# First mixture layer computed from packed rows times w_in, on one core of a Trainium2 chip

## The chip, the core and the metric

One Trainium2 chip, one of its cores. The metric is device time of one execution in microseconds (us); the time of a kernel is the median of its runs. Five engines work side by side, each through its own list in order: PE (TensorE, matmuls; its weight loads are shown as PEld), DVE (VectorE), ACT (ScalarE), POOL (GpSimd) and SP (SyncE, which here issues all transfers).

## What is computed

Attention goes through 32 packed rows per head, twice a softmax; then come two dense mixture layers over 2304 tokens. All is float32, but w_in and w_out arrive as float64.

```python
def sm_attn(qq, kk, vv):
    s = scale * np.matmul(qq, kk.transpose(0, 1, 3, 2))
    s = s - np.max(s, axis=-1, keepdims=True)
    a = np.exp(s)
    a = a / (np.sum(a, axis=-1, keepdims=True) + 1e-09)
    return np.matmul(a, vv)
p_packed = sm_attn(p, k, v)                # (4, 8, 32, 64)
out = sm_attn(q, p_packed, p_packed)       # (4, 8, 576, 64)
x = out.transpose(0, 2, 1, 3).reshape(2304, 512)
h = x @ w_in                               # (512, 2048)
g = h * (1.0 / (1.0 + np.exp(-1.702 * h)))
x = g @ w_out                              # (2048, 512)
p = domain_probs / (domain_probs.sum(-1, keepdims=True) + 1e-09)
for e in range(4):
    h = np.maximum(x @ w1[e], 0.0)         # (512, 1024)
    out2 += p[:, e:e + 1] * (h @ w2[e])    # (1024, 512)
```

## The kernel before

**Attention** is done in eight units, one per batch and group of four heads. `pack(u)` (L230) transposes k, takes scores of the packed rows (L253), the maximum and exponential (L260, L266), transposes the exponentials (L280), multiplies by v (L287) and leaves in `pp` the packed rows, once transposed (L308) and once block-diagonal over head pairs (L300). `unpack(u)` (L312) transposes q, takes scores (L324), the softmax over 32 packed rows (L335 to L343), and multiplies the softmax weights with the packed rows (L348, float32, 288 columns, two records each in the trace). The result is x, features on partitions.

**Precision.** Every large matrix is kept as two parts, high and low, whose sum is the float32 value. A product of the MoE layers is three products: high x high, low x high, high x low (`PARTS`, L17). The split is a rounding copy on ACT and a subtraction. A float64 weight is first turned into float32 by six DVE steps (L155, L156, L160, L166, L169, L172) and one POOL step (L163) for each piece of 128x512; 32 pieces in all. This is called a conversion below. The low part (L99) is made by POOL for the first pass and by DVE later.

**MoE layers.** Tokens are in five blocks (four of 512 columns, one of 256). A pass takes four chunks of 128 hidden columns through all blocks: 4 passes for the first layer, 8 for the second. `f1(i)` (L375) is the first product of a step: 12 matmuls (4 contraction tiles x 3 parts), then the activation on ACT (L397) and the high and low parts on DVE (L398, L399); `f2(i)` (L408) is the second: 12 matmuls into four accumulators (L420, in the second layer L428), added to the block's sum at the pass's end (L454, L465). They are issued as f1(i+1), f2(i), f1(i+2), f2(i+1), so each activation has a step of the other kind as cover.

**Order.** The word list `PROG` (L24) issues loads, stages of pack and unpack, weight fetches (F), conversions (C) and MoE halves (M), and a scheduler sets the order on each engine from it. After the head, `WHEN` (L537) says after which steps the next pass's weights are converted. All loads are on SP, in order; a weight load waits for one of two raw buffers. PSUM has 8 banks, taken in turn.

## Time and profile before

| | |
|---|---|
| runs | 1314.97, 1315.67, 1318.59 us; median 1315.67 |
| profiled execution, span | 1313.9 us from its first to its last instruction; the profile gives no other time of this execution |
| TensorE busy | 1282.4 us, 98% of the span |
| VectorE, ScalarE, GpSimd busy | 524.4, 291.0, 81.8 us |
| mean granted TensorE clock | 0.989 of full speed |
| moved by DMA | 53.71 MB |

The busy time of TensorE is the time with a matmul under way, and a matmul that waits for its predecessor in the array counts as busy. So how fast matmuls follow each other is read from the starts in the timeline, not from the length of one. Idle time of an engine matters only where another one waits for it.

### The profile page before, as it was taken

Reading aid. Unit: us, or ns where it says so; the run is one execution under the profiler, and the core shown is the slowest. Engines: PE = TensorE matmul, PEld = TensorE weight load, DVE = VectorE, ACT = ScalarE, POOL = GpSimd, SP = SyncE. Lnnn points to the kernel's source line nnn. Section 1 sums busy time; section 2 is a strip of 40 time slices with the busy share of each in tenths; the row PEclk is TensorE's granted clock in tenths of the full one; section 3 lists DMA queues with packets and bytes.
Section 4 is the critical chain, followed back from the end, with each engine's and each line's share of the span. In section 5 each row is a group of like instructions: output and inputs, shape, how many; then the busy total and the mean of one; then the engine's idle time right before and its main releaser. Section 6 shows DMA issues by size and latency. Waiting matters only on the chain.

```text
span 1313.9 us, 15157 instructions
## 1 busy us (share of the span) xinstructions
PE 1282.4 (98%) x6400; PEld 1051.0 (80%) x6400; DVE 524.4 (40%) x952; ACT 291.0 (22%) x552; POOL 81.8 (6%) x74
## 2 busy tenths in 40 slices
PE   5699999999999999999999999999999999999998
PEld 4477787888888888888888888888888888888887
DVE  5985559639534453112224223223224224123222
ACT  3555542112111221322112112012112112111110
POOL 2410002101000232000000000000000000000000
PEclk7899999999999999999999999999999999999999
DMA  9662013102101001012001002002002001000011
GB/s 237 164 160 56 19 33 112 49 1 96 32 1 33 0 33 32 0 33 65 0 0 65 0 1 65 0 0 65 0 1 64 0 0 54 11 1 0 33 64 48
DMA packets 79365, 53.71 MB, mean 41 GB/s; under 512 B 43201, under 2 KB 70849, under 8 KB 79297
## 3 DMA queue, kind: packets, MB, share of 16 engines
q1 hardware_dynamic: 79296, 52.74, 14.0%
q8 instruction: 50, 0.82, 0.3%
q14 instruction: 19, 0.15, 0.0%
HBM read 48.01 MB, written 4.72 MB: 40 GB/s over the span
## 4 chain that ended last, share of the span: by engine, by line
PE 92%; DVE 4%; DMA 1%; SPq 1%; POOL 1%; ACT 1%; issue 0%; ACTq 0%; POOLq 0%
PE ps_h L384 45%; PE ps_acc L428 30%; PE ps_acc L420 14%; PE ps_t L220 1%; PE ps_o L348 1%; PE ps_s L324 1%; SPq L212 1%; DVE man L172 1%; DVE ex L169 1%; DMA raw<-in_moe_w_out_dram 0%; POOL ex L163 0%; DVE ex L155 0%; DMA v<-in_v_dram 0%; DMA raw<-in_moe_w_in_dram 0%; DVE w L99 0%
## 5 line engine op out<-in xcount | busy, mean ns | idle before, releaser
L428 PE MATMUL ps_acc<-w,h 128*128 128x512 f32 x1728 | 428.1, 395 | 0.0
L428 PEld LDWEIGHTS ps_acc<-w,h 128*128 128x128 f32 x1728 | 323.6, 189 | 72.7
L402 DVE SCALAR_TENSOR_TENSOR h<-ps_h,h 128x512 fp32r<-128x512 f32 (+1 forms) x160 | 102.2, 639 | 528.9 <-ACT h L401 528.9
L384 PE MATMUL ps_h<-yh,w 128*128 128x512 f32 x1024 | 256.5, 392 | 0.0
L384 PEld LDWEIGHTS ps_h<-yh,w 128*128 128x128 f32 x1024 | 192.3, 188 | 44.4
L401 ACT ACTIVATE h<-ps_h 128x512 fp32r<-128x512 f32 (+1 forms) x160 | 88.8, 555 | 616.1 <-PE ps_h L384 616.1
L420 PE MATMUL ps_acc<-h,w 128*128 128x512 f32 (+1 forms) x960 | 219.8, 375 | 1.5 <-DVE h L398 0.8
L420 PEld LDWEIGHTS ps_acc<-h,w 128*128 128x128 f32 x960 | 167.2, 188 | 38.2 <-DVE h L399 1.7
L384 PE MATMUL ps_h<-yl,w 128*128 128x512 f32 x512 | 137.8, 391 | 0.0
L384 PE MATMUL ps_h<-xh,w 128*128 128x512 f32 x512 | 131.6, 397 | 0.4 <-DVE pp L300 0.4
L384 PEld LDWEIGHTS ps_h<-yl,w 128*128 128x128 f32 x512 | 96.1, 188 | 20.4
L384 PEld LDWEIGHTS ps_h<-xh,w 128*128 128x128 f32 x512 | 95.0, 189 | 21.1 <-PE ps_pt L307 0.7
L397 ACT ACTIVATE g<-ps_h 128x512 f32<-128x512 f32 (+1 forms) x80 | 44.4, 555 | 222.1 <-PE ps_h L384 212.1
L398 DVE CAST h<-g 128x512 fp32r<-128x512 f32 (+1 forms) x80 | 35.5, 444 | 136.7 <-ACT g L397 136.6
L465 DVE SCALAR_TENSOR_TENSOR acc<-ps_acc,pr,acc 128x512 f32<-128x512 f32 x126 | 86.4, 743 | 2.2 <-PE ps_acc L428 2.2
L384 PE MATMUL ps_h<-xl,w 128*128 128x512 f32 x256 | 69.8, 394 | 0.0
L99 DVE TENSOR_TENSOR w<-raw,w 128x1024 fp32r<-128x1024 f32 x32 | 41.7, 1308 | 52.0 <-ACT w L98 52.0
L384 PEld LDWEIGHTS ps_h<-xl,w 128*128 128x128 f32 x256 | 48.5, 190 | 10.3
L399 DVE TENSOR_TENSOR h<-g,h 128x512 fp32r<-128x512 f32 (+1 forms) x80 | 53.5, 669 | 1.6
L384 PEld LDWEIGHTS ps_h<-y,w 128*128 128x128 f32 x384 | 50.3, 191 | 2.8
L384 PE MATMUL ps_h<-y,w 128*128 128x256 f32 x384 | 51.0, 283 | 0.0
L163 POOL TENSOR_SCALAR ex<-ex 128x512 uint32<-128x512 uint32 x32 | 33.4, 1043 | 187.7 <-DVE ex L160 187.6
(82 smaller groups left out, 649.7 us busy)
## 6 DMA issues: line engine op xcount, KB each, us to landing
raw<-in_moe_w_dram SPq DMA_DIRECT2D x64, 256.0 KB, 3.0
raw<-in_moe_w_in_dram SPq DMA_DIRECT2D x16, 512.0 KB, 3.7
raw<-in_moe_w_out_dram SPq DMA_DIRECT2D x16, 512.0 KB, 3.7
k<-in_k_dram SPq DMA_DIRECT2D x32, 144.0 KB, 4.1
v<-in_v_dram SPq DMA_DIRECT2D x8, 576.0 KB, 6.5
q<-in_q_dram SPq DMA_DIRECT2D x32, 144.0 KB, 4.3
out_dram<-acc SPq DMA_DIRECT2D x18, 256.0 KB, 2.0
praw<-in_p_dram SPq DMA_DIRECT2D x1, 256.0 KB, 3.1
```

The lines of the kernel that those rows point to most:

```text
L99: eng.tensor_sub(out=dst[:, 1, :], in0=src, in1=dst[:, 0, :].bitcast(F32))
L163: nc.gpsimd.tensor_scalar(out=ex, in0=ex, scalar1=-float(896 << 20), scalar2=8.0, op0=ALU.add, op1=ALU.mult)
L169: nc.vector.scalar_tensor_tensor(out=ex, in0=hi, scalar=0x80000000, in1=ex, op0=ALU.bitwise_and, op1=ALU.bitwise_or)
L384: nc.tensor.matmul(out=ps[:, :n], lhsT=w[:, wp, kk * 128:(kk + 1) * 128], rhs=x[xp][:, kk, :], start=(m == 0), stop=(m == 3 * KD - 1),)
L397: nc.scalar.activation(out=g32[:, :n], in_=ps[:, :n], func=AF.Gelu_apprx_sigmoid)
L398: nc.vector.tensor_copy(out=h[:, 0, :n], in_=g32[:, :n])
L399: nc.vector.tensor_sub(out=h[:, 1, :n], in0=g32[:, :n], in1=h[:, 0, :n].bitcast(F32))
L401: nc.scalar.activation(out=h[:, 0, :n], in_=ps[:, :n], func=AF.Relu)
L402: nc.vector.scalar_tensor_tensor(out=h[:, 1, :n], in0=ps[:, :n], scalar=0.0, in1=h[:, 0, :n].bitcast(F32), op0=ALU.max, op1=ALU.subtract,)
L420: nc.tensor.matmul(out=accs[j][t][:, :n], lhsT=w[:, wp, 512 + t * 128:512 + (t + 1) * 128], rhs=h[:, hq, :n], start=(c == 0 and m == 0), s ...
L428: nc.tensor.matmul(out=accs[j][t], lhsT=h[:, hq, t * 128:(t + 1) * 128], rhs=w[:, wp, 512:1024], start=(c == 0 and m == 0), stop=(c == CPP ...
L465: nc.vector.scalar_tensor_tensor(out=acc[:, t, :], in0=ps[t], scalar=pr[:, tok, e:e + 1], in1=acc[:, t, :], op0=ALU.mult, op1=ALU.add,)
```

## The change

Since x = A P (A the softmax weights, P the packed rows, block-diagonal over the heads), x w_in = A (P w_in). For each pass and batch, `packed_w` multiplies the transposed block-diagonal packed rows of a unit with 512 columns of w_in; the result, split in two parts, is the stationary operand of `l1_first`, whose moving operand is A^T (four heads x 32 rows = 128 partitions per unit, two units). So a step's first product has 6 matmuls in place of 12, and L348 and its splits go; A is split instead (`split` in `unpack`). The first layer works in eight half-batches of 288 tokens in place of five blocks; the second layer keeps its blocks, and `put_y` writes the first layer's result into them. ACT makes the activation twice (into the rounded high part, and in float32) and DVE only the low part.

All eight packs are in the list ahead of the first MoE step; units 2 to 7 are unpacked beside the first layer's first pass. Slots are 36 small ones instead of 20 large ones, raw buffers three instead of two; w_in is fetched in rows of 512 columns. POOL takes over the low part of every converted piece, the mask product of p, the subtraction of the maximum in `unpack`, and the low parts of the packed rows. In the second layer the next pass's weights are converted after other steps (`WHEN`).

```diff
-    "k0 k1 F F v0 q0 v1 S P1 P0 P1 P1 q1 P0 C P0 P1 P0 P1 P0 P0 P1 P1 P0 k2 v2 C U1 k3 v3 q2 P2 P3 C U0 "
...
+    "k0 k1 S v0 v1 P0 P1 k2 k3 P0 P1 F P0 P1 F v2 v3 P0 P1 P0 P1 C P2 P3 k4 k5 P0 P1 P2 P3 C F v4 v5 P0 P1 P2 P3 C "
...
-    big = ctx.enter_context(tc.tile_pool(name="big", bufs=20))
+    big = ctx.enter_context(tc.tile_pool(name="big", bufs=36))
-    rawp = ctx.enter_context(tc.tile_pool(name="rawp", bufs=2))
+    rawp = ctx.enter_context(tc.tile_pool(name="rawp", bufs=3))
+    cv = ctx.enter_context(tc.tile_pool(name="cv", bufs=2))
...
-        split_w(w[:, :, s * 512:(s + 1) * 512], f32, aux)
+        split(w[:, 0, :], w[:, 1, :], f32, nc.gpsimd)
...
-        nc.vector.scalar_tensor_tensor(
-            out=pp[:, 2:4, :].rearrange("p j (a d) -> p (j a) d", a=2),
...
+        pw = ppws[b][:, g]
+        nc.gpsimd.memset(pw.bitcast(F32), 0.0)
+        for j in range(2):
+            cs = slice(64 * j, 64 * j + 64)
+            split(pw[:, j, 0, cs], pw[:, j, 1, cs], ppT[:, cs], nc.gpsimd)
...
-        nc.vector.tensor_sub(out=t, in0=t, in1=s2[:, 0, :].unsqueeze(2).to_broadcast([128, NB, NP]))
+        nc.gpsimd.tensor_sub(out=t, in0=t, in1=s2[:, 0, :].unsqueeze(2).to_broadcast([128, NB, NP]))
...
+        A[u] = slot([128, 2, S], F32R, f"a{u}")
+        split(A[u][:, 0, :], A[u][:, 1, :], aT, nc.vector)
...
-                nc.tensor.matmul(
-                    out=ps[:, :HS], lhsT=pp[:, 2 + j, :], rhs=aT[:, s * HS:(s + 1) * HS], start=True, stop=True
-                )
...
+    def packed_w(a, b):
+        for g in range(UG):
...
+            for j in range(2):
+                for wp, xp in PARTS:
+                    nc.tensor.matmul(
+                        out=ps, lhsT=pw[:, j, wp, :], rhs=W["in", a, 2 * g + j][:, xp, :],
...
+            split(PW[a, b, g][:, 0, :], PW[a, b, g][:, 1, :], ps, nc.vector)
...
+    def l1_first(a, j, c):
...
+        for wp, xp in PARTS:
+            for g in range(UG):
+                nc.tensor.matmul(
+                    out=ps[:, :HS],
+                    lhsT=PW[a, b, g][:, wp, c * 128:(c + 1) * 128],
+                    rhs=A[b * UG + g][:, xp, s * HS:(s + 1) * HS],
...
+        nc.scalar.activation(out=h[:, 0, :HS], in_=ps[:, :HS], func=AF.Gelu_apprx_sigmoid)
+        nc.scalar.activation(out=g32, in_=ps[:, :HS], func=AF.Gelu_apprx_sigmoid)
+        nc.vector.tensor_sub(out=h[:, 1, :HS], in0=g32, in1=h[:, 0, :HS].bitcast(F32))
...
-    WHEN = ((2, 0), (2, 3), (4, 1), (4, 2))
+    WHEN = ((2, 0), (4, 0), (4, 1), (4, 2))
```

The order on the engines, at three places (a name after the line number is what is written, those behind the arrow what is read).

PE around the first MoE product, before: v products of units 2 and 3 (L287), their last transposes (L307), then the first step of f1 (L384).

```order
L287 MATMUL ps_v<-v_304,k_299 32x64 x24
L287 MATMUL ps_v<-v_335,k_330 32x64 x24
L307 MATMUL ps_pt<-ident,pp_342 128x128
L384 MATMUL ps_h<-xh_548,w_169 128x512 x6
L307 MATMUL ps_pt<-ident,pp_348 128x128
```

The same place now: the last scores of units 6 and 7 (L235), the packed rows times w_in (L347), the exponentials of units 6 and 7 (L262), then their v products (L269); `l1_first` (L362) comes behind those.

```order
L347 MATMUL ps_w<-win,ppw_387 128x512
L235 MATMUL ps_s<-kT_899,pT_811 64x288
L347 MATMUL ps_w<-win,ppw_387 128x512 x5
L262 MATMUL ps_e<-ident,E_988 96x128 x6
L262 MATMUL ps_e<-ident,E_1002 96x128 x6
L347 MATMUL ps_w<-win,ppw_387 128x512 x6
L269 MATMUL ps_v<-v_639,k_539 32x64 x2
```

Four more packs stand ahead of the first product than before.

DVE in the first layer, before, in a stretch with conversions: each L398/L399 pair is an activation's two parts, L99 the low part of a piece of weights.

```order
L99 TENSOR_TENSOR w7_2102<-man_2103,w7_2102 128x512
L169 SCALAR_TENSOR_TENSOR ex_2117<-raw7_1_2070,ex_2117 128x512
L398 CAST h_2142<-g32_2143 128x512
L172 SCALAR_TENSOR_TENSOR man_2116<-man_2116,ex_2117 128x512
L399 TENSOR_TENSOR h_2142<-g32_2143,h_2142 128x512
L398 CAST h_2172<-g32_2173 128x512
```

The same engine now, in a middle pass, behind a packed product (pw0 and pw1 are its low parts, L374 the low part of an activation, L419 the sum of a half-batch, the rest conversion).

```order
L91 TENSOR_TENSOR pw0_2636<-ps_w_2629,pw0_2636 128x512
L91 TENSOR_TENSOR pw1_2646<-ps_w_2639,pw1_2646 128x512
L157 TENSOR_SCALAR man_3010<-raw_2627 128x512
L374 TENSOR_TENSOR h_2656<-g32_2657,h_2656 128x288
L166 SCALAR_TENSOR_TENSOR man_3010<-raw_2627,man_3010 128x512
L157 TENSOR_SCALAR man_3128<-raw_2765 128x512
L172 SCALAR_TENSOR_TENSOR man_3010<-man_3010,ex_3011 128x512
L419 TENSOR_TENSOR acc1_1582<-ps_acc_2575,acc1_1582 128x288
L374 TENSOR_TENSOR h_2680<-g32_2681,h_2680 128x288
```

Steps of two conversions stand between the activations' low parts; L157 writes a buffer that POOL's subtraction of an earlier piece has read.

ACT while queries are unpacked beside the first layer, now (L372 and L373 the two activations, L321 the exponential of a unit, L208 copies of transposed queries).

```order
L208 COPY qT_1159<-ps_t 128x288 x2
L208 COPY qT_1176<-ps_t 128x288 x2
L90 CAST win<-man 128x512
L372 ACTIVATE h<-ps_h 128x288
L373 ACTIVATE g_1262<-ps_h 128x288
L321 ACT_TABLE_LOAD
L321 ACTIVATE t_1231<-t_1231 128x576
L372 ACT_TABLE_LOAD
```

Before, one activation (L397) stood where two stand now; the table loads on both sides of an exponential were there too.

## Rows read from the trace of the kernel before

**Rows 1.** The page, part 1: engine, busy us, share of the span, instructions.

```profile
PE 1282.4 (98%) x6400; PEld 1051.0 (80%) x6400; DVE 524.4 (40%) x952; ACT 291.0 (22%) x552; POOL 81.8 (6%) x74
```

**Rows 2.** The page, part 4: the chain that ended last, by engine.

```profile
PE 92%; DVE 4%; DMA 1%; SPq 1%; POOL 1%; ACT 1%; issue 0%; ACTq 0%; POOLq 0%
```

**Rows 3.** Stretches: length, busy us of each engine (instructions), clock, DMA share, GB/s.

```profile
293.08:392.97 99.89, 99.89 (x481) 83.54 (x481) 59.78 (x116) 15.87 (x28) 8.15 (x8) 1.00 0.13 43
592.82:692.88 100.06, 100.06 (x458) 82.52 (x457) 25.64 (x37) 16.45 (x27) 0.00 (x0) 1.00 0.07 22
62.37:507.40 445.03, 442.67 (x2386) 362.68 (x2387) 257.71 (x522) 132.86 (x270) 57.44 (x49) 1.00 0.18 50
```

**Rows 4.** Timeline: start us, us, engine, line; second products of 512 and 256 columns.

```profile
264.87 2.95 PE L420 MATMUL ps_acc<-h,w 128*128 128x512 f32 x12
...
270.39 2.95 PE L420 MATMUL ps_acc<-h,w 128*128 128x512 f32 x12
...
278.83 1.59 PE L420 MATMUL ps_acc<-h,w 128*128 128x256 f32 x12
...
281.68 1.59 PE L420 MATMUL ps_acc<-h,w 128*128 128x256 f32 x12
```

**Rows 5.** Timeline: the first MoE matmuls, and the last sums.

```profile
62.37 1.85 PE L384 MATMUL ps_h<-xh,w 128*128 128x512 f32 x6
...
1307.88 2.84 DVE L465 SCALAR_TENSOR_TENSOR acc<-ps_acc,pr,acc 128x512 f32<-128x512 f32 x4 [2.17 <-PE ps_acc L428]
```

**Rows 6.** The product L348 after 62.4 us (stretch), and unpack's other matmuls (timeline).

```profile
62.40:240.00 177.60, 13.94 (x48) 8.69 (x48) 11.69 (x37) 10.81 (x36) 0.99 0.30 81
...
106.33 1.16 PE L220 MATMUL ps_t<-ident,q 96*128 96x96 f32 x12
...
114.35 2.16 PE L324 MATMUL ps_s<-qT,pp 128*64 128x288 f32 x16
```

**Rows 7.** Stretches of the head, columns as in rows 3.

```profile
20.00:40.00 20.00, 15.88 (x178) 12.51 (x180) 14.01 (x34) 10.66 (x33) 6.30 (x5) 0.68 1.05 258
40.00:60.00 20.00, 12.14 (x140) 8.43 (x138) 18.65 (x45) 9.63 (x28) 8.10 (x7) 0.74 0.54 130
80.00:100.00 20.00, 19.32 (x186) 13.65 (x185) 16.43 (x43) 14.94 (x33) 3.62 (x4) 1.00 0.60 142
```

**Rows 8.** Conversion: tile ex (stretch), L156 and L166 (groups); L260; L360 in 28:63.

```profile
0.00:1314.00 1314.00, 73.67 (x128) 33.37 (x32) 0.99 0.14 41
...
L166 DVE SCALAR_TENSOR_TENSOR man<-raw,man 128x512 f32<-128x512 uint32 x32 | 23.3, 734 | 0.0
...
L156 DVE TENSOR_SCALAR man<-raw 128x512 uint32<-128x512 uint32 x32 | 13.2, 417 | 0.0
...
L260 DVE TENSOR_REDUCE st<-ps_s 128x1 f32<-128x288 f32 x16 | 6.9, 444 | 1.3 <-PE ps_s L253 1.1
...
L360 DVE TENSOR_TENSOR xl<-ps_o,xh 128x288 fp32r<-128x288 f32 (+2 forms) x12 | 3.8, 348 | 0.0
```

**Rows 9.** Timeline: L172 beside POOL's subtraction, and without one.

```profile
17.33 1.77 POOL L99 TENSOR_TENSOR w<-man,w 128x512 fp32r<-128x512 f32 x1
18.01 1.64 DVE L172 SCALAR_TENSOR_TENSOR man<-man,ex 128x512 f32<-128x512 f32 x1
...
31.67 0.69 DVE L172 SCALAR_TENSOR_TENSOR man<-man,ex 128x512 f32<-128x512 f32 x1
```

**Rows 10.** Groups by shape: busy us, mean ns, idle before; activation, low parts, table load.

```profile
L399 DVE TENSOR_TENSOR h<-g,h 128x256 fp32r<-128x256 f32 x16 | 7.8, 486 | 0.5
...
L397 ACT ACTIVATE g<-ps_h 128x512 f32<-128x512 f32 x64 | 38.3, 598 | 182.3 <-PE ps_h L384 172.3 <-issue 4.8 <-DVE h L399 4.6
...
L397 ACT ACTIVATE g<-ps_h 128x256 f32<-128x256 f32 x16 | 6.1, 383 | 39.8 <-PE ps_h L384 39.8
...
L397 ACT ACT_TABLE_LOAD x7 | 9.0, 1283 | 4.2 <-PE ps_h L384 4.1
...
L99 POOL TENSOR_TENSOR w<-man,w 128x512 fp32r<-128x512 f32 x8 | 11.2, 1399 | 10.2 <-ACT w L98 10.0
```

More of the change, by code (lines that the diff above doesn't have):

```diff
@@ L130, in fetch_w @@
[L130 to L138 removed]
+                out=raw[:, 0, :].rearrange("p (k f) -> p k f", k=KD),
+                in_=w1[e][:, fs].rearrange("(k p) f -> p k f", p=128),
+            )
+            nc.sync.dma_start(out=raw[:, 1, :], in_=w2[e][fs, :])
+            raws[key] = raw
+            return
+        raw = rawp.tile([128, 512, 2], U32, tag="raw", name="raw")
@@ L139, in make_piece, with make_w @@
+        flat = raw.rearrange("p f two -> p (f two)")
+        if kind == "in":
+            src = w_in.bitcast(U32)[c * 128:(c + 1) * 128, a * 1024:(a + 1) * 1024]
+        else:
+            r0 = (a * CPP + c) * 128
+            src = w_out.bitcast(U32)[r0:r0 + 128, :]
+        nc.sync.dma_start(out=flat, in_=src)
+        raws[key] = raw
+    def make_w():
+        if state["cvt"] >= len(pieces):
+            return
+        key = pieces[state["cvt"]]
         state["cvt"] += 1
-        if ("w", i, s) not in raws:
+        if key not in raws:
@@ L141, in make_piece @@
             fetch_w()
-        raw = raws.pop(("w", i, s))
-        if s == 0:
-            W[i] = big_tile([128, 2, 1024], F32R, f"w{i}")
-        w = W[i]
-        if halves(i) == 1:
-            split_w(w, raw, nc.vector)
+        raw = raws.pop(key)
+        if key[0] == "x":
+            for s in range(2):
+                w = W["x", key[1], s] = slot([128, 2, 512], F32R, f"w{s + 1}")
+                split(w[:, 0, :], w[:, 1, :], raw[:, s, :], nc.vector)
             fetch_w()
             return
+        w = W[key] = slot([128, 2, 512], F32R, "w" + key[0])
@@ L373, in packed_attention_moe_kernel @@
     ACC = {}
-    def f1(i):
-        a, j, c = steps[i]
+    Y = {}
+    def packed_w(a, b):
+        for g in range(UG):
+            pw = packed[b * UG + g][1]
+            ps = psum("ps_w")
+            m = 0
+            for j in range(2):
+                for wp, xp in PARTS:
+                    nc.tensor.matmul(
+                        out=ps, lhsT=pw[:, j, wp, :], rhs=W["in", a, 2 * g + j][:, xp, :],
+                        start=(m == 0), stop=(m == 5),
+                    )
+                    m += 1
+            PW[a, b, g] = slot([128, 2, 512], F32R, f"pw{g}")
+            split(PW[a, b, g][:, 0, :], PW[a, b, g][:, 1, :], ps, nc.vector)
+            yield
@@ new lines, in put_y @@
+    def put_y(t, tok, n, src):
+        done = 0
+        while done < n:
+            jb = max(i for i in range(len(blocks)) if blocks[i][0] <= tok + done)
+            b0, bn = blocks[jb]
+            o = tok + done - b0
+            w = min(n - done, bn - o)
+            if (jb, t) not in Y:
+                m = 512 // bn
+                tile_ = slot([128, m, 2, bn], F32R, f"y{jb}_{t}")
+                for x in range(m):
+                    Y[jb, t + x] = tile_[:, x]
+            y = Y[jb, t]
+            split(y[:, 0, o:o + w], y[:, 1, o:o + w], src[:, done:done + w], nc.gpsimd)
+            done += w
@@ new lines, in l2_first @@
+    def l2_first(a, j, c):
+        h = hid.pop((a, j, c))
+        if c == 0:
+            accs[j] = [psum("ps_acc") for _ in range(KD)]
+        for t in range(KD):
+            for m, (wp, hq) in enumerate(PARTS):
+                nc.tensor.matmul(
+                    out=accs[j][t][:, :HS],
+                    lhsT=W["out", a, c][:, wp, t * 128:(t + 1) * 128],
+                    rhs=h[:, hq, :HS],
+                    start=(c == 0 and m == 0),
+                    stop=(c == CPP - 1 and m == 2),
+                )
+            if t == 1:
+                yield
+        if c == CPP - 1:
+            ps = accs.pop(j)
+            if a == 0:
+                ACC[j] = slot([128, KD, HS], F32, f"acc{j}")
+            for t in range(KD):
+                dst = ACC[j][:, t, :]
+                if a == 0:
+                    nc.scalar.copy(out=dst, in_=ps[t][:, :HS])
+                else:
+                    nc.vector.tensor_add(out=dst, in0=ps[t][:, :HS], in1=dst)
+                if a == n_pass1 - 1:
+                    put_y(t, j * HS, HS, dst)
+        yield
```

402 lines of the change are left out of this document (174 added, 228 removed), and 8 rows, old and new, of tables (HEAD, PROG).

## The prediction

> **What bounds the kernel now.** I read the busy line first, then the chain, then stretches. The busy line shows TensorE at 98% and VectorE at 40% [rows 1]; the chain that ended last is 92% TensorE [rows 2]. The reader should see two regimes. From the first MoE matmul at 62.37 us to the end of the last one, just before 1307.88 us [rows 5], TensorE is nearly never without work: in 62.37 to 507.40 it is busy 442.67 of 445.03 us, at clock 1.00 [rows 3]. So there only TensorE work counts. One pass of the first layer takes 99.89 us (four passes: 399.6) and one of the second 100.06 (eight: 800.5) [rows 3]. Together that is 1200.1 of the 1245.5 us after 62.37; the other 45.4 us is attention work still open then. Before 62.37 the kernel waits: in 40 to 60 us TensorE is busy 12.14 of 20 us, VectorE 18.65 [rows 7]. There VectorE and the loads decide.
>
> **First-layer matmuls.** A 24-matmul step of 512 columns repeats after 5.52 us and one of 256 after 2.85 us [rows 4]: 230 and 118.8 ns a matmul. The trace has no 288-column matmul of this type. Its bounds are 118.8 (if something other than columns set the 256 case) and 118.8 x 288/256 = 133.7; I interpolate to 132.7, since it lies next to the 256 case.
> - The x-by-w_in product shrinks from 12 matmuls per 128 hidden columns and block to 6 of 288: 4 x 8 x 4 x 6 = 768, or 101.9 us.
> - The w_out product keeps its columns but is cut in 288s: 1536 x 132.7 ns = 203.8 us.
> - New: the packed rows times w_in, 4 x 4 x 2 x 6 = 192 matmuls of 512 columns: 44.2 us.
> - Sum 349.9 against 399.6: **-49.7 us**.
>
> **Attention.** The product of softmax weights with packed rows (L348) is gone. The 48 records after 62.4 us took 13.94 us [rows 6]. What is left of an unpack is 12 transposes (1.16 us) and 8 score records (half of the 16 that took 2.16 us) [rows 6]: 2.24 us each, 13.5 for the six units that still follow the first product. With 0.5 for two leftover transposes of the packs, 14.0 us stays behind the first product where 45.4 stood: **-31.4 us**. But only 13.9 of it is removed; the rest moved ahead.
>
> **The first product comes later.** All eight packs, and by VectorE's list also ten whole weight conversions and the front parts of two more, now stand ahead of it; before it was four packs and seven conversions. A conversion costs VectorE 73.67/32 + 0.417 + 0.734 = 3.45 us [rows 8], so three more and 3.2 us of parts are 13.6 us. Four more packs (two maxima of 0.444 each, scaling and small steps, 1.8 each) are 7 us, about what VectorE sheds in masks and copies moved to GpSimd and ScalarE and in the L360 splits (3.8 us [rows 8]). The splits of two softmax blocks and two products add 3. VectorE was 93% busy in the last 20 us before the first product [rows 7], so 16 us more work appears as about 16 to 18 us of time: first product at **80 us**, **+17.6**. Two packed products (2.8 us) are done before that, under the waits, so 347.1 us of the 349.9 remain behind it. Bounds: 72, if the conversions find gaps; 95, if the loads rule. SP's queue matters for the latter: each weight load waits for a free raw buffer, now three instead of two, and the key and value loads of units 6 and 7 stand behind such loads. The loads needed before the first product are about 15 MB (eighteen of 0.59 MB for keys, values and two queries, nine of 0.52 for weights), at 258 GB/s [rows 7] 58 us, so the loads alone need not reach 80.
>
> **New waits inside the first layer.** I price two, and take the smaller effects at nothing.
> (a) While units 2 to 7 are unpacked, ScalarE alternates between exponentials and the first layer's activation. Its list for the first 15 steps has 13 table loads at 1.283 us, 30 activations of 288 columns, now two per step, 36 copies of that size at 0.41, 12 pieces of 576 at 0.65, 8 of 512 at 0.60 and small ones (durations by column count from [rows 10]): 58 us. TensorE needs 15 x 18 x 132.7 ns + 13.5 + 5.5 = 55 us for that stretch. ScalarE, never a limit before, becomes one. If never idle it costs 3 us; at its highest earlier load under cover, 14.94 of 20 us [rows 7], 77 us and so 22. I take 85%, **+13**, as it waits in order on VectorE and GpSimd for each exponential.
> (b) From the second pass on, two conversions follow each packed product. GpSimd now does every low-part subtraction (1.399 us [rows 10]); VectorE's next conversion step waits for it, and the low half of an activation stands right behind that. The row to see first: L172 took 1.64 us, starting inside a 1.77-us GpSimd subtraction, and 0.69 without one [rows 9]. So VectorE instructions stop while GpSimd subtracts. Between the end of one product group and the use of its low half TensorE has 20 matmuls of 288, 2.65 us; the chain is two ScalarE passes of 0.41 and 0.45 on VectorE ([rows 10], scaled by columns), leaving 1.2 us. Behind a packed product stand the casts of its two results and of one piece (1.4 us), two GpSimd subtractions (2.8) and the low half (0.45), 4.8 with hand-offs; it is needed after 26 matmuls, 3.45 us: at most 1.4 us per batch, over the eight batches in whose lists this stands. I take 1.0 each, **+8**; bounds 0 and 11.
>
> The Trainium skill, page SBUF — State Buffer, section Who interferes with whom, says that a VectorE instruction with two SBUF inputs and a GpSimd one that reads SBUF fully block each other, the second to start waiting for the first. By that rule the low halves (two SBUF inputs) would be blocked too, for up to 1.4 us each time; [rows 9] agree for L172. By that rule the sum takes 31 us in place of the 8, which is the rival *blocked each time* below.
>
> **What costs nothing.** Narrower slots and the larger third buffer are space only. Loads in the second layer keep their work; its passes convert on VectorE and ScalarE as before, where VectorE is busy 25.64 of 100.06 us [rows 3]. Its 800.5 us stand, if weights still come in time: in the new placement each slot is freed some six half-steps of 2.76 us before its new weight is used, about 16 us, against 2 us of conversion. A last-pass split on GpSimd also sits under cover. After the last matmul 6.0 us remain as before (1313.9 - 1307.9).
>
> **Sum.** 80 + 347.1 + 14.0 + 800.5 + 6.0 = 1247.6; with 13 + 8 it is 1268.6 us of span, against the profiled 1313.9. The median of the runs, 1315.67, is 1.8 above that span, so I forecast **1270 us**, 3.5% less. About 0.3% is what a measurement can tell from no change.
>
> **Rivals.**
> - *Cover holds.* The new waits hide as VectorE's conversions did before, when the stretch to 507.40 lost only 2.4 us [rows 3]. Then the first product at 78 and 3 us of waits give 1250. For it: 20 matmuls of cover. Against: ScalarE's 58 against 55. Chance 0.22.
> - *Head late.* The head is bound by the SP queue and conversions together, first product at 95: 1285. For: 11 weight loads interleaved with the eight packs' loads. Against: bandwidth. Chance 0.16.
> - *Blocked each time.* Each of the 22 conversions after the first product has one GpSimd subtraction, and each stops an activation's low half for its whole 1.4 us, with no slack left to take it: 31 us for (b), so 1293. For: [rows 9], and 1.2 us of slack at most. Against: the subtractions run beside other steps too. Chance 0.05.
> - *Slower: conversions stop the first layer.* Each of 22 conversions after the first product holds VectorE for its 3.45 us plus a blocked 1.4, with activations queued behind, and TensorE's 1.2 us of slack is gone at once: 3.7 us each, 81 us in all, plus (a): 1343. It decides from (1313.9 - 1247.6 - 13)/22 = 2.4 us a conversion. For: VectorE would be at 70 to 80% in these batches, far above the pass's 59.78 of 99.89 us [rows 3]. Against: the list puts single steps, not whole conversions, ahead of an activation. Chance 0.05.
> - *The clock falls.* Waits of microseconds in the first layer bring TensorE from 2.4 to 1.2 GHz, as in 20 to 40 us, where the mean granted clock is 0.68 with TensorE busy 15.88 of 20 [rows 7]. All of its 350 us at that level would add up to 350: 1600; slower as soon as 45 us of it run so. Against: the 256-column blocks ran within a pass at 1.00 [rows 3]. Chance 0.03. The Trainium skill, page TensorE: Matmul & The Clock Gate, section HAM oscillation — how this bites in real kernels, advises for thin matmuls a loop that keeps the contraction tiles together or padding M to 512 and more, so that TensorE stays at full clock; read for these blocks that speaks against 288, and the rows of the 256 blocks show no such loss.
> - *The change doesn't do what it says*, the saved product being hidden anyway: excluded by the busy share, except as far as waits replace it: same time, 0.03.
>
> **How the numbers follow.** The forecast case, waits between 10 and 35 us, has 0.46: 1257 to 1284. The range 1244 to 1302 takes in the held cover, the late head and the bounds of (a) and (b), and leaves out the slower cases and the far end of the head: about 0.15. Faster: 0.46 + 0.22 + 0.16 + 0.05 = 0.89; same 0.03; slower 0.08.
>
> **What would show it.** Right: no L348 successor; 768 + 1536 matmuls of 288 columns at 130 to 135 ns; a middle pass of the first layer of 88 to 91 us instead of 99.89; passes of the second layer at 100.06; the first 288-column product near 80 us; TensorE waits of 10 to 30 us in the first layer, named after the ScalarE activations and the VectorE low halves. Wrong: a clock below 1.00 there, passes over 95 us, or a head beyond 95 us.

## The result and the profile after

The changed kernel takes 1285.01 us (median of four runs, 1284.71 to 1286.69) against 1315.81 in the same comparison: ratio 0.9762, 95% interval 0.9748 to 0.9776, so 2.4% faster. The forecast was 1270 us in a range of 1244 to 1302: right in direction and in range, 15 us too low. The profiled execution has a span of 1282.5 us; the forecast's sum for it was 1268.6.

Busy line and chain of the changed kernel, which answer to [rows 1, 2]:

```profile
PE 1219.0 (95%) x6912; PEld 1052.8 (82%) x6912; DVE 496.2 (39%) x919; ACT 353.8 (28%) x816; POOL 137.9 (11%) x166
...
PE 80%; issue 3%; DVE 2%; POOL 2%; ACT 0%; DMA 0%; POOLq 0%; DVEq 0%; ACTq 0%
```

TensorE's busy time fell by 63.4 us, the span by 31.4: half of the gain went into waits. Next, from the timeline of TensorE (start, length, what) and the chain (start, length), the rows that cut the span into stages:

```profile
93.89 0.53 PE L362 MATMUL ps_h<-a,pw 128*128 128x288 f32 x2
...
235.01 2.76 PE ps_w L347 x12
258.17 2.77 PE ps_w L347 x12
...
374.44 2.77 PE ps_w L347 x12
396.34 2.77 PE ps_w L347 x12
...
548.50 2.75 PE ps_o L464 x12
...
647.27 2.75 PE ps_o L464 x12
...
1276.56 2.81 DVE o L485 x4
```

The first 288-column product starts at 93.89. A packed product opens each batch: most batches with conversions take 23.16 us, those without 21.90. The second layer repeats after 98.77 us (548.50 to 647.27), eight times 790.2. TensorE ends at 1276.56; what is left between is the first layer, with the attention beside it.

| stage, us | before | forecast | measured |
|---|---|---|---|
| up to the first product | 62.4 | 80 | 93.9 |
| first layer, attention and waits beside it | 445.0 | 347.1 + 14 + 21 = 382.1 | 392.5 |
| second layer | 800.5 | 800.5 | 790.2 |
| after the last matmul | 6.0 | 6.0 | 5.9 |
| span | 1313.9 | 1268.6 | 1282.5 |

So three terms missed, two by +14 and +10, one by -10, and the last two cancel by luck. TensorE's waits from 94 us to the second layer (line waited at, whom for: us in total, times, longest):

```profile
PE ps_acc L401 <- DVE h L374: 12.3, 13, 2.0
PE ps_acc L401 <- ACT h L372: 4.5, 2, 3.5
PE ps_h L362 <- DVE t L315: 1.8, 1, 1.8
PE ps_acc L401 <- ACT g L373: 1.6, 1, 1.6
PE ps_h L362 <- DVE pw L91: 0.9, 2, 0.7
```

They are 21.1 us, where the forecast had 21. Of the first row, this part lies in 180 to 420 us:

```profile
PE ps_acc L401 <- DVE h L374: 8.3, 8, 1.2
```

The head, in stretches of 20 us (busy time and count of PE, PEld, DVE, ACT, POOL; clock; DMA share; GB/s), which answers to [rows 7]:

```profile
20.00:40.00 20.00, 10.58 (x90) 7.58 (x90) 12.81 (x29) 5.97 (x18) 7.83 (x7) 0.57 0.98 248
40.00:60.00 20.00, 11.48 (x164) 9.00 (x164) 15.54 (x33) 9.46 (x33) 12.32 (x15) 0.83 0.95 231
60.00:80.00 20.00, 10.48 (x151) 8.06 (x151) 13.67 (x33) 7.90 (x28) 10.47 (x13) 0.66 0.91 227
```

The engines are far from full, the transfers at 0.91 to 0.98. The longest TensorE waits there are three of 5.7 to 8.9 us, each behind ScalarE. The third, from the timeline:

```profile
67.74 0.99 POOL L290 MEMSET ppw<- 128x512 f32 x2
68.29 0.85 ACT L90 CAST ppw<-ppT 128x64 fp32r<-128x64 f32 x4 [8.01 <-POOL ppw L290]
...
69.05 0.99 ACT L208 COPY qT<-ps_t 128x288 f32<-128x288 f32 x3
69.50 1.70 PE L207 MATMUL ps_t<-ident,q 96*128 96x96 f32 x9 [8.69 <-ACT qT L208]
```

A cast stands at the head of ScalarE's list for 8.01 us, until GpSimd, itself behind a conversion step, has zeroed its tile; the copy that TensorE needs stands behind it.

### The profile page after: what moved, and what is told of

Read it like the earlier page. It is cut to its first block, busy times and chain, and to the rows that moved or that the text cites. A ratio compares the mean times of both kernels' runs of the same rounds, so it can differ in the third digit from the quotient of the medians.

```text
span 1282.5 us, 16591 instructions
## 1 busy us (share of the span) xinstructions
PE 1219.0 (95%) x6912; PEld 1052.8 (82%) x6912; DVE 496.2 (39%) x919; ACT 353.8 (28%) x816; POOL 137.9 (11%) x166
## 4 chain that ended last, share of the span: by engine, by line
PE 80%; issue 3%; DVE 2%; POOL 2%; ACT 0%; DMA 0%; POOLq 0%; DVEq 0%; ACTq 0%
PE ps_g L436 31%; PE ps_o L464 31%; PE ps_acc L401 11%; PE ps_h L362 5%; PE ps_w L347 2%; POOL y L91 1%; POOL wout L91 1%; DVE h L374 0%; POOL ex L163 0%; DVE man L157 0%; DMA raw<-in_moe_w_out_dram 0%; DVE o L485 0%; POOL t L325 0%; DVE ex L156 0%; DVE acc L419 0%
## 5 line engine op out<-in xcount | busy, mean ns | idle before, releaser
L464 PE MATMUL ps_o<-w,h 128*128 128x512 f32 x1728 | 421.7, 392 | 0.0
L436 PE MATMUL ps_g<-y,w 128*128 128x512 f32 (+1 forms) x1920 | 420.3, 368 | 0.0
L436 PEld LDWEIGHTS ps_g<-y,w 128*128 128x128 f32 x1920 | 338.6, 188 | 63.3
L464 PEld LDWEIGHTS ps_o<-w,h 128*128 128x128 f32 x1728 | 322.5, 188 | 67.9
L448 DVE SCALAR_TENSOR_TENSOR h<-ps_g,h 128x512 fp32r<-128x512 f32 (+1 forms) x160 | 102.1, 638 | 505.3 <-ACT h L447 505.3
L401 PE MATMUL ps_acc<-h,wout 128*128 128x288 f32 x1536 | 234.7, 300 | 18.6 <-DVE h L374 12.3
L447 ACT ACTIVATE h<-ps_g 128x512 fp32r<-128x512 f32 (+1 forms) x160 | 88.8, 555 | 586.4 <-PE ps_g L436 586.4
L401 PEld LDWEIGHTS ps_acc<-h,wout 128*128 128x128 f32 x1536 | 215.2, 191 | 24.2 <-DVE h L374 15.7
L362 PE MATMUL ps_h<-a,pw 128*128 128x288 f32 x768 | 124.5, 297 | 2.7 <-DVE t L315 1.8
L362 PEld LDWEIGHTS ps_h<-a,pw 128*128 128x128 f32 x768 | 110.0, 188 | 5.9 <-ACT pw L90 2.0
L372 ACT ACTIVATE h<-ps_h 128x288 fp32r<-128x288 f32 x128 | 52.7, 412 | 148.4 <-PE ps_h L362 148.2
L374 DVE TENSOR_TENSOR h<-g,h 128x288 fp32r<-128x288 f32 x128 | 60.8, 475 | 70.9 <-ACT g L373 70.5
L373 ACT ACTIVATE g<-ps_h 128x288 f32<-128x288 f32 x128 | 52.2, 408 | 0.0
L419 DVE TENSOR_TENSOR acc<-ps_acc,acc 128x288 f32<-128x288 f32 x96 | 39.0, 449 | 23.6 <-PE ps_acc L401 23.6
L347 PE MATMUL ps_w<-win,ppw 128*128 128x512 f32 x192 | 48.0, 395 | 0.0
L347 PEld LDWEIGHTS ps_w<-win,ppw 128*128 128x128 f32 x192 | 34.9, 188 | 8.0 <-issue 0.4
L163 POOL TENSOR_SCALAR ex<-ex 128x512 uint32<-128x512 uint32 x32 | 30.0, 936 | 97.1 <-DVE ex L160 92.9
L91 DVE TENSOR_TENSOR pw<-ps_w,pw 128x512 fp32r<-128x512 f32 x32 | 21.9, 689 | 36.3 <-ACT pw L90 36.3
```

Source lines behind the costliest of these rows:

```text
L91: eng.tensor_sub(out=lo, in0=src, in1=hi.bitcast(F32))
L347: nc.tensor.matmul(out=ps, lhsT=pw[:, j, wp, :], rhs=W["in", a, 2 * g + j][:, xp, :], start=(m == 0), stop=(m == 5),)
L362: nc.tensor.matmul(out=ps[:, :HS], lhsT=PW[a, b, g][:, wp, c * 128:(c + 1) * 128], rhs=A[b * UG + g][:, xp, s * HS:(s + 1) * HS], start=(m ...
L372: nc.scalar.activation(out=h[:, 0, :HS], in_=ps[:, :HS], func=AF.Gelu_apprx_sigmoid)
L373: nc.scalar.activation(out=g32, in_=ps[:, :HS], func=AF.Gelu_apprx_sigmoid)
L374: nc.vector.tensor_sub(out=h[:, 1, :HS], in0=g32, in1=h[:, 0, :HS].bitcast(F32))
```

## Experiments on the head: what holds the first product at 94 us

The runs below stand in several comparisons, in which the kernel before has medians of 1315.45 to 1316.76 us, and the head of the changed kernel, run again all but unchanged in e5_low_dve, ends at 94.94 instead of 93.89. So differences of 1 to 2 us in time, or 1 us in the head, are not read as effects.

All three of those waits were attacked first, as they add up to 23 us.

**Zeroing early** (e1_ppw_early):

```diff
+        if g == 0:
+            ppws[b] = slot([128, UG, 2, 2, 128], F32R, f"ppw{b}")
+        nc.gpsimd.memset(ppws[b][:, g].bitcast(F32), 0.0)
...
         ps = psum("ps_pt")
...
-        nc.gpsimd.memset(pw.bitcast(F32), 0.0)
```

> The zeroing of the block-diagonal packed rows (ppw, GpSimd) and the claim of its slot move from the end of a pack to its beginning; nothing else changes. Theory A (ScalarE's list is blocked from its head): in the changed kernel ScalarE stood 4.91 and 8.01 us with a ppw cast at the head of its list, because the zeroing stood on GpSimd behind conversion steps that waited for VectorE; the exponentials and query copies that TensorE waited for (5.7 and 8.7 us) stood behind that cast. With the zeroing done early both waits go: first 288-column product at 80 to 84 us instead of 93.9, time 1271 to 1275. Theory B (the loads rule the head, the queues at 0.90 to 0.98 share until 80 us): TensorE waits for k, v or q transfers in place of ScalarE, the first product stays above 90 us, time 1282 to 1285. In between: VectorE's list is late next, product at 86 to 90, time 1277 to 1281.

Measured: 1285.4 us, ratio 0.9767 (0.9752 to 0.9782); first product at 97.78. The 8.69-us wait shrank to 1.7 and the 5.7-us one to 1.1, and others grew: 13.2 us for the exponentials' copies on ScalarE instead of 8.9, 3.1 for VectorE.

**First conversion later** (e2_first_conv_later):

```diff
-"... v2 v3 P0 P1 P0 P1 C P2 P3 k4 k5 P0 P1 P2 P3 C F ..."
+"... v2 v3 P0 P1 P0 P1 P2 P3 k4 k5 P0 P1 C P2 P3 C F ..."
```

> Only the first weight conversion (C) is moved nine words later in the head's list, behind the key loads of units 4 and 5 and the next six stages of packs 0 to 3. In the changed kernel VectorE stood 6.65 us and ScalarE 8.77 us for the transfer of that piece at 18 to 27 us, and the copy of the transposed exponentials of unit 1 stood behind it on ScalarE; TensorE waited 8.9 us. Theory A: that wait goes, the first product comes up to 8.9 us earlier (85 to 87 us), time 1276 to 1279. Theory B (VectorE's total or the loads rule the head): the same work is only later in the list, the first product stays within 2 us of 93.9, time 1283 to 1287; or the postponed conversion is missed later and the time rises up to 3 us.

Measured: 1284.86 us, ratio 0.9758 (0.9745 to 0.9772); first product at 95.58. The 8.9-us wait is gone, one of 12.3 for VectorE's scaling (L277) has come.

**Both** (e3_both, the two diffs together):

> Both edits of the two runs before: early zeroing of ppw, and the first conversion nine words later. Theory A (the three ScalarE waits, 23 us together, are what the forecast of 80 us left out): first product at 72 to 79 us, time 1262 to 1270. Theory B (loads): TensorE waits for transfers, first product above 88 us, time above 1279. If VectorE's total is next, as the forecast's step had it, the first product is at 79 to 82 and the time 1270 to 1274.

Measured: 1287.05 us, ratio 0.9772 (0.9759 to 0.9786); first product at 94.84. Theory A falls: the waits named in a trace were 23 us, and taking their causes away gave nothing. The 8.9-us wait and the 8.69-us one are gone (1.0 and 0.5 are left), but where the 5.7 stood there are 5.90, now behind a cast that waits for a conversion step, and one of 11.20 for VectorE's scaling has come. TensorE waited for transfers 1.4 us only, so B is not shown in its own form; but ahead of that scaling VectorE itself stood 6.7 and 1.8 us for loads of weights, so it is not excluded either.

**Less to load** (e7_v_reused, which leaves out the loads of v for units 4 to 7):

```diff
+        if name == "v" and u >= 4:
+            raws[name, u] = v_kept[u - 4]
+            return
```

> Leaves out the loads of v for units 4 to 7 (eight transfers, 2.36 MB): these units are multiplied with v of units 0 to 3. Every engine's instructions are as in the changed kernel, so only the loads differ. Theory B (the loads rule the head): 2.36 MB at 235 GB/s are 10 us, first product at 84 to 88 us, time 1275 to 1279. Theory C (the engines' waits on each other rule it): first product at 91 to 95, time 1282 to 1286.

Measured: 1280.97 us, ratio 0.9736 (0.9721 to 0.9750); first product at 91.77, though the transfers' share in 20 to 80 us fell from 0.95 to 0.81. Ten us less of transfers gave 2.1 in the head: C's place, with a time between the two.

**Conversions cut to one step** (e10_short_conv, for the first pass's eight pieces only):

```diff
+        if key[1] == 0:
+            nc.vector.tensor_scalar(out=man, in0=hi, scalar1=0xFFFFF, scalar2=0x100000, ...)
+        else:
             ...
```

> Leaves out six of the seven steps of each conversion for the eight pieces of the first pass (L156, L160, L163, L166, L169, L172; only L157, the rounding cast and the subtraction stay), so the weights of that pass are not the reference's. All loads, packs and their order stay. Theory D (conversions set the pace of the head: in 57 to 70 us a conversion's L157 follows the last after 5.3 and 7.3 us instead of the 3.45 that the forecast gave it, through VectorE, GpSimd, VectorE and the wait for the subtraction): eight conversions at 2 to 3 us less than forecast and more, first product at 68 to 78 us, time 1259 to 1270. Theory B (loads): 0.95 of the transfer time until 80 us is used already, first product at 85 to 92, time 1276 to 1284. Theory E (the packs' own chains through five engines): first product above 90.

Measured: 1282.98 us, ratio 0.9742 (0.9728 to 0.9755); first product at 96.38. Stretch 20 to 80 us of this run, to be set against the sum of the three rows of the changed kernel above:

```profile
20.00:80.00 60.00, 33.07 (x403) 24.83 (x404) 17.72 (x53) 22.49 (x76) 19.35 (x27) 0.66 0.93 232
```

VectorE has 24.3 us less to do (17.72 for 42.02) and the first product is no earlier. That ends the forecast's own view, in which VectorE's added work was the head's added time. It does not show that nothing but the packs' chains is left: VectorE now waits for loads. Its waits for transfers in 20 to 80 us, changed kernel, then this run:

```profile
DVE ex L156 <- DMA raw<-in_moe_w_in_dram: 7.4, 3, 6.7
```

```profile
DVE man L157 <- DMA raw<-in_moe_w_in_dram: 14.7, 3, 6.0
DVE man L157 <- DMA raw<-in_moe_w_out_dram: 13.8, 3, 5.9
DVE ex L161 <- DMA raw<-in_moe_w_in_dram: 6.2, 1, 6.2
```

They are 34.7 us for 7.4. The last of them is the ninth piece, one of the second pass, which keeps all its steps. GpSimd's step of that conversion (68.51) stands ahead of the zeroing (69.18), and so the third of the waits above is there again and longer; from the timeline:

```profile
69.74 0.85 ACT L90 CAST ppw<-ppT 128x64 fp32r<-128x64 f32 x4 [14.37 <-POOL ppw L295]
...
70.94 1.70 PE L212 MATMUL ps_t<-ident,q 96*128 96x96 f32 x9 [12.00 <-ACT qT L213]
```

From the query copies at 70.49 the chain that ended last goes on for 26 us (two of its pieces; lines of this run's file, five more than in the changed kernel):

```profile
86.86 1.17 POOL t L330
...
94.76 1.69 PE ps_v L274 x96
```

Up to 88.8 us these are mostly the copies, scores and softmax of the first two queries (here L213 to L332), one step after the other through ScalarE, VectorE and GpSimd, each in line with stages of packs 4 to 7; the rest are the exponentials and products of packs 6 and 7, which stand ahead of the first product on TensorE. In the changed kernel the same stretch, from the copies at 69.05 to 93.89, is 24.8 us.

**Packs 4 to 7 behind the first product** (e6_packs_late):

```diff
-"... q0 q1 P2 P3 P4 P5 C k6 k7 P2 P3 P4 P5 C v6 v7 ... U0 U1 P6 P7 M ..."
+"... q0 q1 P0 P1 P2 P3 C F ... C U0 U1 P2 P3 C k4 k5 U0 U1 ... U0 U1 C M M M M U2 M U3 ... M P4 M P5 ..."
```

> Only the word list of the head changes: packs 4 to 7, with their key and value loads, stand beside the first pass of the first layer again instead of ahead of it, as in the kernel before; the packed product and all else stay. Three edits of the head left the first product at 94 to 98 us, so what bounds the head moved from engine to engine. Theory B (the loads rule: 0.88 to 0.98 of the transfer time until 80 us): 4.7 MB less ahead of the first product at 235 GB/s are 20 us, first product at 72 to 78 us; 6 to 9 us of pack work on TensorE come back behind it, with waits for ScalarE in the first pass: time 1270 to 1282. Theory C (VectorE and ScalarE set the pace of the head by their waits on each other): the four packs' 1.8 us each on VectorE go, first product at 84 to 88, and the same work returns in the first pass: time 1283 to 1292.

Measured: 1293.36 us, ratio 0.9826 (0.9811 to 0.9840). TensorE's timeline:

```profile
82.22 3.49 PE L364 MATMUL ps_h<-a,pw 128*128 128x288 f32 x12 [24.27 <-ACT pw L92]
```

The first product comes 11.7 us sooner and the kernel is 8.4 us slower. The packed product had been ready for 24.27 us; its cast stood on ScalarE behind the casts of all eight conversions. That cast alone did not hold it: the softmax weights that the first product reads were rounded at 79.35 to 81.16 us. So an earlier first product is no gain in itself: work that is moved behind it is paid there.

**A list with half of both ahead** (e13_late_only; five conversions, the fifth right ahead of it, and four packs stand before the packed product; the others follow between the first layer's steps):

```diff
+"... C U0 U1 P2 P3 U0 U1 C P2 P3 U0 U1 P2 P3 U0 U1 P2 P3 N q2 q3 U0 U1 C M M M C M M M C M M M C M U2 M U3 k4 k5 ..."
```

> The new word list of the 1264.8-us version alone, with all low parts on GpSimd as in the changed kernel. It parts that version's gain of 20.2 us into list and low parts (the low parts alone gave 13.9) and asks what an earlier first product is worth. Theory 1 (the two are independent): first product at 60 to 61 us, time 1278 to 1280. Theory 2 (in the longer first pass, with packs beside it, GpSimd's subtractions stop VectorE at worse places): time 1282 to 1288, waits of TensorE for the low halves 12 us or more after 94 us. Theory 3 (VectorE was the limit there and the low parts took its time): with them off VectorE the list alone gives more than 6.3, time below 1277.

Measured: 1276.92 us, ratio 0.9711 (0.9696 to 0.9726), 8.1 us less than the changed kernel; first product at 61.88. Waits for the low halves are 9.7 us in 180 to 480, much as before, so theory 2 falls. Theory 1 (1278 to 1280) and theory 3 (below 1277) can't be told apart with runs of 1276.33 to 1279.68. The 32 us in the head gave 8 in the end. In 60 to 80 us VectorE is busy 19.48 of 20, some steps stretched beside GpSimd: with this list it looks like the limit, which no run tests.

What holds the changed kernel's head is thus not one engine's total. As the traces read, loads to 70 us, conversions beside them, and a softmax that stands in line with four packs all end near the same time; taking away those waits, a part of the loads or most steps of the conversions, each by itself, moved the first product by -2 to +4 us, and only a shorter list ahead of it moved it far.

## Experiments on the waits in the first layer

**Low parts on VectorE again from the second pass** (e5_low_dve):

```diff
-        split(w[:, 0, :], w[:, 1, :], f32, nc.gpsimd)
+        split(w[:, 0, :], w[:, 1, :], f32, nc.gpsimd if key[1] == 0 else nc.vector)
```

> One part of the change undone: the low part of the pieces of the second to fourth pass (24 of 32) is subtracted on VectorE again instead of GpSimd; the first pass's eight stay on GpSimd. In the changed kernel TensorE waited 8.3 us in 180 to 420 us, eight times, for the low half of an activation, which stood behind a conversion step that waited for GpSimd's subtraction. Theory A (wait for GpSimd, and the two engines stopping each other): the 8.3 us fall under 2, passes of 90.5 us or less, time 1276 to 1279. Theory B (VectorE has simply too many steps ahead of the low half): VectorE's own 0.73 us per piece comes to stand there too, the waits stay 6 to 12 us, time 1283 to 1288.

Measured: 1271.08 us, ratio 0.9655 (0.9642 to 0.9668), 13.9 us less than the changed kernel. Stretch 180 to 420 us, changed kernel and this run:

```profile
180.00:420.00 240.00, 231.70 (x1634) 224.26 (x1634) 133.45 (x271) 88.17 (x230) 42.69 (x38) 1.00 0.14 40
```

```profile
180.00:420.00 240.00, 239.88 (x1708) 233.99 (x1707) 144.64 (x301) 93.64 (x246) 20.28 (x27) 1.00 0.14 43
```

VectorE does 11 us more and TensorE waits 8.2 us less: every batch there now takes 21.9 us. Between the first product and 180 us TensorE waits 10 us for the changed kernel's 12.8. One part of the change, meant to unload VectorE, cost 13.9 us.

**More buffers for the conversion** (e4_man4):

```diff
-    big = ctx.enter_context(tc.tile_pool(name="big", bufs=36))
+    big = ctx.enter_context(tc.tile_pool(name="big", bufs=35))
-        man = cv.tile([128, 512], U32, tag="man", name="man")
+        man = cv.tile([128, 512], U32, tag="man", bufs=4, name="man")
```

> The conversion's mantissa buffer (man) gets four copies instead of two; to make room there are 35 slots instead of 36. All subtractions stay on GpSimd. It parts the two readings of what the return of the low parts to VectorE gave (waits of 8.3 us in 180 to 420 us down to none, 1271.08 us). Theory A1 (buffer wait: the conversion step L157 waits until GpSimd has read the old man, and the low half stands behind it): the waits named after L157 and the eight waits of TensorE go, time 1271 to 1276. Theory A2 (the engines stop each other while GpSimd subtracts): the low halves and steps of VectorE still stretch, TensorE still waits 5 us or more in 180 to 420 us, time 1280 to 1286.

Measured: 1286.47 us, ratio 0.9773 (0.9759 to 0.9788); TensorE still waits 7.3 us in 180 to 420 us. Timeline of the changed kernel, of e4_man4, and of e5_low_dve (start, length, what, idle before it):

```profile
262.41 2.53 POOL L91 TENSOR_TENSOR wout<-man,wout 128x512 fp32r<-128x512 f32 x2 [11.90 <-ACT wout L90]
263.75 1.48 DVE L157 TENSOR_SCALAR man<-raw 128x512 uint32<-128x512 uint32 x1 [1.46 <-POOL wout L91]
265.14 0.45 DVE L374 TENSOR_TENSOR h<-g,h 128x288 fp32r<-128x288 f32 x1
265.64 0.53 PE L401 MATMUL ps_acc<-h,wout 128*128 128x288 f32 x2 [1.25 <-DVE h L374]
```

```profile
240.43 2.53 POOL L91 TENSOR_TENSOR win<-man,win 128x512 fp32r<-128x512 f32 x2 [10.73 <-ACT win L90]
241.76 1.49 DVE L157 TENSOR_SCALAR man<-raw 128x512 uint32<-128x512 uint32 x1 [1.20 <-POOL win L91]
243.17 0.45 DVE L374 TENSOR_TENSOR h<-g,h 128x288 fp32r<-128x288 f32 x1
243.67 0.53 PE L401 MATMUL ps_acc<-h,wout 128*128 128x288 f32 x2 [1.01 <-DVE h L374]
```

```profile
254.78 0.46 DVE L374 TENSOR_TENSOR h<-g,h 128x288 fp32r<-128x288 f32 x1
255.16 0.42 DVE L157 TENSOR_SCALAR man<-raw 128x512 uint32<-128x512 uint32 x1
```

With four buffers L157 waits by its semaphore for the subtraction of four pieces earlier, which ended a batch ago. It still starts only when GpSimd's first subtraction ends (240.43 + 1.29 = 241.72) and lasts 1.49 us, through the second; without GpSimd it takes 0.42. The releaser in the bracket is inferred; by the four buffers it is not a semaphore wait here. So the buffer was not the cause (A1 falls): VectorE's instruction itself is stopped while GpSimd subtracts, the low half L374 behind it is late, and TensorE waits. Seven of the eight waits in 180 to 420 us stand behind an L157 of 1.48 to 1.50 us; at the eighth (0.63 us, at 228.61) the low half itself took 0.87 us for its 0.45 beside GpSimd's step L163.

The Trainium skill, page SBUF — State Buffer, section Who interferes with whom, lists tensor_scalar among the operations that can take both of VectorE's SBUF ports, and then VectorE and GpSimd block each other for a whole instruction. The trace agrees: L157 is a tensor_scalar with one SBUF input, 0.42 us alone and 1.49 beside a subtraction.

## The second layer, and a faster version

The second layer's matmuls are as before, yet its pass is 1.3 us shorter. TensorE's timeline there, kernel before and changed kernel:

```profile
703.83 2.96 PE L428 MATMUL ps_acc<-w,h 128*128 128x512 f32 x12
706.62 2.01 PE L384 MATMUL ps_h<-yh,w 128*128 128x512 f32 x8
708.47 1.08 PE L384 MATMUL ps_h<-yl,w 128*128 128x512 f32 x4
709.38 2.96 PE L428 MATMUL ps_acc<-w,h 128*128 128x512 f32 x12
```

```profile
704.90 2.88 PE L436 MATMUL ps_g<-y,w 128*128 128x512 f32 x12
707.62 2.91 PE L464 MATMUL ps_o<-w,h 128*128 128x512 f32 x12
710.36 2.88 PE L436 MATMUL ps_g<-y,w 128*128 128x512 f32 x12
```

Start to start, twelve matmuls of the first product take 2.76 us before (706.62 to 709.38) and 2.72 now, of the second 2.79 and 2.74. The clock is 1.00 in both, and twelve of 256 columns take 1.43 to 1.44 in both.

**Two tries to find it in the kernel before**: e9_before_w_layout puts high and low part of 512 columns side by side, e12_before_pitch sets the slots further apart.

```diff
-            W[i] = big_tile([128, 2, 1024], F32R, f"w{i}")
+            W[i] = big_tile([128, 2, 2, 512], F32R, f"w{i}")
...
+            for x in range(2):
+                split_w(w[:, x], raw[:, x * 512:(x + 1) * 512], nc.vector)
...
```

> The kernel before with one part of the change: the weights of a chunk stand as two tiles of 512 columns, each with its high and low part side by side, and the second layer splits them in two instructions of 512 columns instead of one of 1024. It asks why a 512-column matmul of the second layer follows the last after 226.7 and 229 ns in the changed kernel and 230 and 233 ns in the kernel before, 10 us over the layer, while the 256-column ones take the same. If the place of the weights' parts (or the length of the splitting instructions) does it: 12 matmuls in 2.72 and 2.75 us instead of 2.76 and 2.80, time 1303 to 1308. If not: 2.76 and 2.80 stay, time 1313 to 1318.

```diff
-    big = ctx.enter_context(tc.tile_pool(name="big", bufs=20))
+    big = ctx.enter_context(tc.tile_pool(name="big", bufs=19))
-            W[i] = big_tile([128, 2, 1024], F32R, f"w{i}")
+            W[i] = big_tile([128, 2, 1088], F32R, f"w{i}")[:, :, :1024]
```

> The kernel before with its large slots 8704 instead of 8192 bytes apart (19 instead of 20, for space; a chunk's low part then starts 4352 bytes behind its high part). It asks again why a 512-column matmul takes 226.7 and 229 ns in the second layer of the changed kernel and 230 and 233 in the kernel before. If the distance of the slots does it (4608 bytes in the changed kernel, 8192 before): 12 matmuls in 2.72 and 2.75 us, and 8 to 10 us less in the second layer. If not: 2.76 and 2.80 us stay. One slot less can cost some waits, time 1305 to 1325.

Measured: 1315.99 us (ratio 0.9998, 0.9988 to 1.0007) and 1317.5 (1.0011, 1.0002 to 1.0020); 2.76 and 2.80 us in both. In every variant of the changed kernel it is 2.72 and 2.75. Weight layout and length of the splits are excluded, and so is the slot distance as far as 512 bytes more can tell. A candidate is left that no run tested, the place of y, the second layer's input: in the kernel before, its high and low part lay in two tiles for the blocks of 512 tokens and in one for the block of 256, and a step of that block takes 2.82 us before and 2.83 now; the changed kernel has both parts in one tile everywhere. What gives these 10 us stays open.

**Both gains together** (e11_late_and_dve: the list of e13 and the low parts of e5):

> A try at a faster version: the low parts of the second to fourth pass on VectorE (as in the run at 1271.08 us), and a new word list for the head in which only four conversions and half of the packs stand ahead of the packed product; the last four conversions follow one to each step of the first layer, packs 4 to 7 and the unpacks of units 2 to 7 stand beside the first pass. The run with packs 4 to 7 late had TensorE wait 24.3 us for the cast of the packed product, which stood behind all eight conversions on ScalarE. If that order was the fault: first product at 60 to 66 us, some 10 to 15 us of new waits in the first pass for the second product's weights, time 1250 to 1262. If VectorE's total rules until the first pass is through, the time is 1266 to 1275: the waits only move behind the first product.

Measured: 1264.8 us, ratio 0.9605 (0.9592 to 0.9618): 20.2 us less than the changed kernel. The head list alone gave 8.1 and the low parts alone 13.9, together 22.0, so they are nearly independent. Its stretch 60 to 80 us:

```profile
60.00:80.00 20.00, 14.58 (x84) 12.86 (x84) 20.00 (x32) 7.21 (x15) 9.22 (x9) 0.84 0.30 88
```

VectorE is busy for all 20 us, with conversions for the most part: the next gain may lie there, which was not tried.

## Why the prediction was right or wrong

- **First-layer matmuls: right.** A batch without conversions takes 21.90 us; the forecast's 349.9 us over 16 batches is 21.87. Twelve matmuls of 288 columns take 1.60 us from start to start, 133.3 ns each for the forecast's 132.7:

```profile
484.95 1.76 PE L401 MATMUL ps_acc<-h,wout 128*128 128x288 f32 x12
486.55 2.93 PE L436 MATMUL ps_g<-y,w 128*128 128x512 f32 x12
```

  The two middle passes take 94.0 and 91.6 us, from packed product to packed product (210.56, 304.60, 396.18), a little over the 88 to 91 that were to show it: their waits are (b), below.
- **Attention: right in the main.** No successor of L348 is there. Behind the first product 72 query transposes are busy 8.69 us, 48 score records 7.15 and two leftover transposes 0.38, together 16.2 for the forecast's 14.0; lengths of matmuls overlap, so this is an upper bound.
- **The first product comes later: wrong, 93.9 for 80.** The step took VectorE's added work, 16 us, as added time, since VectorE was 93% busy in the last stretch before [rows 7]. In the changed kernel it is busy 13.67 of 20 us in 60 to 80 and 16.86 in the last 20 before its first product, and 24 us less work for it moved nothing (e10). The step left out that the list puts the first queries' softmax, a chain of 25 us, in line with four packs whose last load lands at 70. Its estimate for the loads alone, 58 us for 15 MB, was too low as well: over the first 70 us the transfers run at a mean of 239 GB/s, which is 16.7 MB. The rival *head late* had the place (95) and the time (1285) almost exactly; it named SP's queue and the conversions together. Fewer loads or fewer conversion steps, each alone, gave 2 us or none, which does not refute it: with the conversions cut, VectorE stood 34.7 us for loads. Both at once, and nothing else, was not tried; e13, with an earlier first product by 32 us, takes loads, conversions and packs away from the head together.
- **(a) 13 us: size right, cause half right.** Waits from 93.9 to 180 us are 12.8: 6.1 for ScalarE, 6.7 for VectorE. ScalarE is busy 14.52 of 20 us at most (94 to 114), 73% and not 85. But the first layer came out 10.4 us longer than the forecast although the waits are as forecast. A part is the rival *clock falls*, in small, and a sign that the forecast had named for being wrong. TensorE's timeline, then two stretches of 4 us:

```profile
113.90 0.53 PE L401 MATMUL ps_acc<-h,wout 128*128 128x288 f32 x2 [1.61 <-ACT g L373]
116.39 4.69 PE L401 MATMUL ps_acc<-h,wout 128*128 128x288 f32 x18 [1.96 <-DVE h L374]
120.87 0.36 PE L207 MATMUL ps_t<-ident,q 96*128 96x96 f32 x1
```

```profile
114.00:118.00 4.00, 2.04 (x9) 1.81 (x10) 2.89 (x7) 1.28 (x3) 1.29 (x2) 0.71 0.08 18
118.00:122.00 4.00, 4.00 (x20) 3.99 (x20) 1.83 (x4) 2.27 (x6) 0.00 (x0) 0.50 0.00 0
```

  After two waits of 1.61 and 1.96 us with 0.53 of work between them, the granted clock is 0.50, the 1.2-GHz level, and 18 matmuls take 4.48 us instead of 18 x 132.7 ns = 2.39. After the wait of 3.5 us at 143 us it falls again. The clock costs some 4.5 us by this reckoning (an estimate): 2.1 here, 0.9 in the twelve transposes and matmuls behind, and 1.5 in the 14 matmuls from 143.18 to 146.58. A wait also costs more than its row: the six batches from 235.01 to 374.44 take 139.4 us, 8.0 more than six of 21.90, and their six waits are 6.5, so 0.26 more for each. For the first pass's 11 waits that is some 2.9 us; the eight waits of (b) cost 10.4 in this way, 2.4 over the forecast's 8. Together 9.8 of the 10.4, some 7 of them in the first pass.
- **(b) 8 us: right in size and place.** 8.3 us, eight waits, 1.2 at most, seven of them at the low half behind L157. The forecast named both GpSimd's buffer and the stopping of VectorE; the runs leave only the second. The rival *blocked each time* (31 us) fell: in seven of eight L374 is late behind L157, not stretched itself. Without these subtractions on GpSimd the kernel is 13.9 us faster (e5), more than (b), as some stand beside the first pass too.
- **Second layer "what costs nothing": wrong by -10.3 us.** The 800.5 us were taken over as the passes' code did not change. 790.2 were measured. That is luck: it hides the first layer's 10.4, so that the forecast's 14 us too few look like the head's alone.
- The Trainium skill, page TensorE: Matmul & The Clock Gate, section HAM oscillation — how this bites in real kernels, advises against thin M because of the waits between its short bursts of matmuls. The trace agrees on the waits: the clock fell only where TensorE had waited. It shows no loss from the width itself: the 288-column blocks run at clock 1.00 from 180 to 420 us, TensorE busy 231.70 of 240.

## What to carry to other kernels

A named wait is not a price: the causes of three waits, 23 us in the head, were taken away and the time stayed, because other waits moved up where each engine's list and the loads ended near the same point; look for what else arrives just behind before counting a wait as a gain. Moving elementwise work from a half-idle engine to an idle one can cost time where the two stop each other: 0.7 us per piece taken off VectorE cost TensorE 13.9 us. And a first product that comes earlier is worth only what isn't then paid behind it (11.7 us earlier was 8.4 slower, 32 us earlier 8.1 faster).
